# A new opening order, two more expert weight pieces ahead and other fillers in an attention and mixture-of-experts kernel

## The chip, the cores and the metric

The kernel runs on one core of one Trainium2 chip. The metric is the device time of one execution in microseconds. TensorE is PE in the profile, VectorE is DVE, ScalarE is ACT, GpSimd is POOL; SP issues the DMAs.

## The reference, cut to what matters

```python
# 1. chunked attention, 4 x 8 heads of 768 x 64: chunks of 32 queries, 16 keys of
#    left and 8 of right context and 8 memory keys
scores = scale * q_c @ k_full.T            # k_full = mem_k and the window
a = exp(scores - scores.max(-1)); a /= a.sum(-1) + 1e-9
out[chunk] = a @ v_full
# 2. heads side by side: x is 3072 tokens x 512
h = x @ w_in                               # 512 -> 2048
x = (h * sigmoid(h)) @ w_out               # 2048 -> 512
# 3. soft mixture of 8 experts with 4 slots each
logits = x @ phi                           # 512 -> 32 slots
d = exp(logits - logits.max(0)); d /= d.sum(0) + 1e-9      # over all tokens
slot_in = d.T @ x                          # 32 x 512
slot_out[e] = relu(slot_in[e] @ w1[e]) @ w2[e]             # 512 -> 1024 -> 512
c = exp(logits - logits.max(1)); c /= c.sum(1) + 1e-9      # over the slots
return c @ slot_out
```

## The kernel before, in words

The 3072 tokens are 24 groups of 128, and these are seven blocks of 256, 384, 384 and four times 512 tokens. Part 2 runs over steps (block j, slice f): `emit_h` makes 128 of the 2048 hidden values of a block (12 matmuls, in which weight and input are split into a high and a low part, L328), `g_tanh`, `g_mult`, `g_hi` and `g_lo` make the activation and its two parts on ACT and DVE, and `emit_y` adds the slice's share to the block's y (three matmuls for every 128 tokens, L357). Blocks 0 and 1 take turns in the first 32 steps, so step 2f is block 0 and 2f + 1 is block 1 with slice f; after that one block follows another. The two weights arrive in 16 slices with 512 KB each; `conv`, `conv_hi` and `conv_lo` (L189 to L222) bring them from a 64-bit layout into a high and a low fp32 part on ACT and DVE, in four operations and two.

The first 32 steps and the attention of the first groups are ordered by hand, word by word, in `OPENING` (L26). A word is a call with its arguments. `q.g`, `v.g`, `w.f.part`, `i` and `p` issue loads on SP's queue (608 KB for q, 512 KB for v and w, the constants, phi; part 0 is w_in and part 1 w_out). `c.f.s.parts` is one of the four conversion operations, `C` and `D` make the high and the low part. For group g, `S` are the scores (64 small matmuls), `M` the maxima and `U` their subtraction (DVE), `E` the exponential (ACT), `O` the sums and `N` the reciprocals (DVE), `Q` the product (POOL for p, DVE for v), `T` the four transposes, `A` their copy (ACT), `V` the values (64 small matmuls), `X` and `Y` the high and the low part (ACT, DVE). `h.i.bank`, `s.i`, `t.i`, `u.i`, `l.i`, `y.i` are the six parts of step i. `z.n.bank` are n filler matmuls. Every engine runs its own instructions in the order of the words, and so does SP with the loads: a load that waits for its buffer holds up the loads behind it. Groups 0 and 1 are block 0, groups 2 to 4 block 1, so step 1 needs V, X and Y of groups 2, 3 and 4 only.

The loads of groups 1 to 4 lie in the places that later take the weight slices: q.1 and v.1 in those of slices 14 and 13, q.2 and v.2 in 12 and 11, q.3 and v.3 in 10 and 9, q.4 and v.4 in 8 and 7 (`EARLY`, L137). The raw slice f is loaded to its own place (slice 0 to that of 15).

`keep_warm` (L172) issues filler matmuls into a bank that nothing reads; 21 of them stand ahead of the opening (L582), others around the last block's routing (L674 to L692).

`route` (L382) does the slot logits of a block, the running maximum and sum over the tokens, and adds d.T @ y to `acc`. For the last block it is spread over L626 to L702. There `c_turn` (L498) transposes four tiles of the combine weights into a bank and copies them back on ACT ("a") or DVE ("v"). `siz` is the slots' input, spread out for the experts. After it come the experts: `expert1` and `relu`, `to_hT`, `expert2`, `slot_out`, `combine` and the stores of the output.

The expert weights are 64 pieces with 512 KB, pieces 0 to 31 of w1 and 32 to 63 of w2. `load_ew` (L518) puts the next n of `ew_order` into a freed place, and `reload_ew` (L535) does that again as soon as the experts have read all of a place; when no piece is left the place goes to `ew_free`. During the last block the places are those of x0 (4 pieces, at its first step) and of the weight slices (2 each, one step after another); after its last step x1 (4), the last slices, two halved pieces in the activation buffers (`load_ew_halves`, L530) and st1 (2). That makes 44 pieces ahead of the experts.

Of the kernel before, what the change touches and what calls it, by code (L numbers as in the profile page):

```python
# [7 lines left out]
F32 = mybir.dt.float32  # L8
# [18 lines left out]
w.0.0 c.0.1.0 c.0.2.0 q.2 S.2.7.6 M.2 c.0.0.0 q.0 q.3 U.2 c.0.3.0 E.2 O.2 v.3 N.2 S.3.5.2 q.4 M.3 C.0.a.0 q.1 w.0.1  # L27
U.3 S.0.0.1 i S.4.7.6 v.2 E.3 M.0 S.1.5.2 O.3 w.1.0 N.3 U.0 c.0.1.1 M.4 Q.2.p U.4 w.1.1 E.0 T.2.0 A.2.a Q.3.p T.3.1
O.0 A.3.a M.1 N.0 c.0.0.1 E.4 V.3.0.7 U.1 O.4 V.2.6.1 E.1 N.4 c.1.1.0.1 w.3.1 v.4 v.1 X.3 Q.0.p Q.4.p T.4.5 c.1.0.0.1
T.0.2 O.1 v.0 N.1 A.4.a c.0.2.1 V.4.3.4 w.2.1 A.0.a Q.1.p w.2.0 c.0.3.1 T.1.5 Y.3 c.1.2.0.1 D.0.v.0 X.2 V.0.7.0 A.1.a  # L30
c.1.3.0.1 X.4 w.6.1 C.0.a.1 w.4.0 c.2.1.0.1 Y.2 C.1.a.0.1 V.1.2.5 Y.4 X.0 D.0.v.1 X.1 w.7.1 h.1.3 D.1.v.0.1 w.4.1
w.3.0 c.2.0.0.1 w.8.0 Y.1 h.3.4 w.13.0 s.1 Y.0 c.4.1.0.1 w.5.1 t.1 h.0.3 u.1 c.4.0.0.1 c.2.2.0.1 l.1.v w.8.1 s.3 s.0
w.5.0 c.2.3.0.1 t.0 y.1 w.6.0 h.2.3 C.2.a.0.1 t.3 u.3 D.2.v.0.1 u.0 c.3.1.0.1 l.0.v s.2 h.4.4 c.5.0.0.1 l.3.v t.2
c.3.2.0.1 c.4.2.0.1 h.5.3 u.2 c.3.0.0.1 w.7.0 l.2.v c.7.1.0.1 c.3.3.0.1 c.4.3.0.1 y.0 s.4 C.3.a.0.1 t.4 c.5.1.0.1 s.5
C.4.a.0.1 D.3.v.0.1 t.5 c.5.2.0.1 y.3 u.4 u.5 l.4.v l.5.v y.2 h.6.4 s.6 c.8.1.0.1 c.5.3.0.1 h.7.3 D.4.v.0.1 s.7
C.5.a.0.1 t.6 c.7.0.0.1 u.6 D.5.v.0.1 w.11.1 w.14.0 y.5 t.7 w.10.1 h.8.4 c.6.1.0.1 l.6.v s.8 y.4 w.15.1 w.9.0 h.10.3
w.11.0 c.7.2.0.1 u.7 t.8 v.5 u.8 l.7.v c.7.3.0.1 s.10 h.9.4 t.10 l.8.v c.6.0.0.1 c.8.0.0.1 s.9 w.10.0 y.6 u.10
C.7.a.0.1 c.6.2.0.1 h.11.3 c.6.3.0.1 q.5 c.10.1.0.1 t.9 y.8 C.6.a.0.1 D.7.v.0.1 l.10.v c.10.2.0.1 c.10.0.0.1 w.9.1
h.14.4 y.10 D.6.v.0.1 y.7 u.9 l.9.v c.8.2.0.1 s.11 t.11 w.14.1 w.12.0 h.12.3 c.10.3.0.1 u.11 c.11.1.0.1 s.12
c.8.3.0.1 l.11.v c.9.1.0.1 t.12 s.14 u.12 c.11.2.0.1 c.9.0.0.1 C.10.a.0.1 t.14 y.9 c.14.1.0.1 c.9.2.0.1 l.12.v h.13.3  # L40
c.9.3.0.1 s.13 w.12.1 D.10.v.0.1 h.15.4 C.8.a.0.1 u.14 y.11 t.13 u.13 h.21.3 l.13.v s.21 l.14.v C.9.a.0.1 D.8.v.0.1
t.21 y.12 u.21 c.14.2.0.1 h.16.3 s.15 c.11.0.0.1 t.15 y.13 c.11.3.0.1 h.17.4 w.13.1 l.21.v c.13.1.0.1 s.16 t.16 u.15
c.12.1.0.1 D.9.v.0.1 p C.11.a.0.1 l.15.v w.15.0 S.5.7.3 y.14 M.5 s.17 U.5 u.16 c.12.0.0.1 t.17 y.15 E.5 D.11.v.0.1
O.5 l.16.v h.18.3 u.17 h.20.4 l.17.v N.5 s.18 c.13.2.0.1 t.18 s.20 y.17 c.12.2.0.1 t.20 c.12.3.0.1 c.13.0.0.1 u.18
C.12.a.0.1 Q.5.p T.5.7 h.22.3 y.16 u.20 l.18.v h.19.4 s.22 A.5.v c.13.3.0.1 q.6 y.18 C.13.a.0.1 l.20.v s.19 t.22
V.5.7.3 t.19 c.15.1.0.1 h.23.4 D.12.v.0.1 c.14.0.0.1 u.19 y.20 c.15.2.0.1 X.5 l.19.v s.23 Y.5 c.14.3.0.1 t.23 u.22
y.19 D.13.v.0.1 u.23 C.14.a.0.1 S.6.7.3 c.15.0.0.1 l.23.v v.6 h.24.4 M.6 s.24 U.6 y.21 t.24 l.22.v E.6 h.26.3
D.14.v.0.1 O.6 u.24 c.15.3.0.1 s.26 h.25.4 l.24.v s.25 t.26 N.6 y.22 Q.6.v h.28.3 T.6.7 A.6.a u.26 C.15.a.0.1 t.25
q.7 h.27.4 l.26.v s.28 y.23 t.28 u.25 l.25.v s.27 t.27 V.6.7.3 y.24 u.28 X.6 D.15.v.0.1 Y.6 y.25 u.27 h.30.4 l.27.v
S.7.7.3 M.7 s.30 U.7 v.7 y.27 h.29.3 y.26 E.7 t.30 u.30 l.28.v O.7 h.31.4 s.29 N.7 Q.7.p t.29 T.7.7 u.29 A.7.a y.28  # L50
l.29.v s.31 t.31 u.31 l.31.v V.7.3.7 X.7 l.30.v Y.7 y.29
# [4 lines left out]
def attn_moe_softmoe_kernel(  # L56
# [12 lines left out]
    nc = tc.nc  # L69
# [38 lines left out]
    ident = cst[:, 0:128]  # L108
# [6 lines left out]
    warm = [call[:, 0:4].rearrange("p t s -> p (t s)").bitcast(mybir.dt.bfloat16)]  # L115
# [3 lines left out]
    def bank(b, shape, name):  # L119
        if b is None:  # L120
            return mbank(shape, name)
        return psum.tile(shape, F32, tag=f"b{b}", name=name)
# [49 lines left out]
    def keep_warm(n, b=0):  # L172
        pw = bank(b, [128, 256], "ps_warm")
        for _ in range(n):
            nc.tensor.matmul(pw, warm[0][:, 0:128], warm[0], start=True, stop=True)
# [331 lines left out]
    ew_order = [*range(28, 32), *range(28), *range(32, 64)]  # L507
# [70 lines left out]
    with tc.manual_schedule():  # L578
        nc.vector.memset(call[:, 0:4], 0.0)
        nc.vector.memset(s_run, 0.0)  # L580
        nc.scalar.activation(out=s_run, in_=s_run, func=ACTF.Exp)
        keep_warm(21)  # L582
# [14 lines left out]
        warm[0] = ident.bitcast(mybir.dt.bfloat16)  # L597
# [5 lines left out]
        for i in range(step_of[2, 0], len(steps)):  # L603
            j, f = steps[i]
            if f == 2 and j < 4:
                misc[0] = [5, 6, 7] if j == 2 else [6, 7]
            if j == NB - 1 and f == 0:
                lctx.close()
                c4_p = ctx.enter_context(tc.tile_pool(name="c4", bufs=1, side="right", reuse_waits="tile"))
                c4.append(c4_p.tile([128, NT, 128], F32R, name="c4"))  # L610
                load_ew((x_p, "x0", 4))
            emit_h(i, 3 + i % 2)
            run(2 * i)
            g_tanh(i)
            g_mult(i)
            g_hi(i)
            g_lo(i, "v")
            emit_y(i - LAG, (0, 1, 2) if i == len(steps) - 1 else None)
            if j == NB - 1 and LAG <= f < NF - 1:
                load_ew((wring, f"w{f - LAG}", 2))  # L620
            run(2 * i + 1)
        assert not slots
        L = NB - 1
# [20 lines left out]
        load_ew((wring, f"w{NF - 1}", 2))  # L644
        load_ew_halves(("gl", {}), ("gl", {}))
        load_ew_halves(("gl", {}), ("g", {"bufs": 2}))
        nc.scalar.activation(out=y[:, 3, 0:256], in_=y_t[L][3][:, 0:256], func=ACTF.Copy, scale=0.5)
# [23 lines left out]
        siz = [g_p.tile([128, 2, 8, 32], F32, tag="gh", name="siz") for _ in range(2)]  # L671
        for t in siz:
            nc.gpsimd.memset(t, 0.0)
        route(L, 4, lambda: (c_turn(8, 1, "a"), c_turn(12, 2, "a"), keep_warm(5, 1)))  # L674
        route(L, 5)
        c_turn(16, 4, "v")
        keep_warm(2, 1)
# [10 lines left out]
        keep_warm(5, 4)  # L688
        psi = mbank([128, 4, 32], "ps_si")
        for c in range(4):  # L690
            nc.tensor.matmul(psi[:, c], acc[:, 128 * c:128 * c + 128], seln, start=True, stop=True)
        keep_warm(4, 4)  # L692
        for c in range(4):
            nc.vector.tensor_copy(
                out=bass.AP(
                    tensor=siz[c // 2].tensor, offset=siz[c // 2][:, c % 2].offset, ap=[siz[c // 2].ap[0], [36, 8], [1, 4]]
                ),
                in_=psi[:, c].rearrange("p (e s) -> p e s", e=8),
            )
# [85 lines left out]
        to_hT(0, hs0, st_tile(2, [128, 8, 128], F32, "hT"))  # L785
# [5 lines left out]
        pool, tag, _ = ew_free.pop(0)  # L791
        to_hT(1, hs1, pool.tile([128, 8, 128], F32, tag=tag, name="hT"))
# [87 lines left out]
```

## Time and profile before

| | us |
|---|---|
| median of 3 runs | 711.75 (710.59 to 714.34) |
| profiled execution, its own time | 713.54 |
| span in its trace | 711.7 |
| PE busy | 686.2 (96%), 6445 matmuls |
| DVE, ACT, POOL busy | 335.3, 251.9, 32.2 |
| mean granted clock of TensorE | 0.972 |
| moved by DMA | 85.29 MB, mean 120 GB/s |

The page cuts the span into forty equal slices and gives each engine's busy share in tenths: TensorE is at 9 from the third slice to the last but one. Matmuls are pipelined and their ends modelled, so a busy TensorE is not one at its peak. The granted clock stands beside, 1.00 for 2.4 GHz and 0.50 for 1.2 GHz. The chain of waits is followed back from the last instruction: each piece is what the next one had to wait for, and "issue" is time in which an engine waited for nothing that the profile shows. In the timeline the brackets give the idle time before an instruction and what ended it.

### The profile page before, as it was taken

What the parts mean: (1) busy time and instruction counts of PE and PEld (TensorE: products, weight loads), DVE (VectorE), ACT (ScalarE), POOL (GpSimd) and SP (SyncE); (2) the same over time, 40 slices, a digit from 0 to 9 for tenths busy, and PEclk for the clock granted to TensorE, in tenths of its full rate; (3) what the DMA queues carried; (4) which work ended last, traced back from release to release, by engine and by line L of the source; (5) the groups of instructions that cost most, each with busy time, mean ns of one, the idle gap of its engine ahead of it and who ended that gap; (6) DMA issues with size and microseconds to landing.
All of it is one profiled execution on the core that took longest, in us unless ns stands there. A gap on an engine that the chain in (4) does not pass through costs nothing.

```text
span 711.7 us, 14737 instructions
## 1 busy us (share of the span) xinstructions
PE 686.2 (96%) x6445; PEld 551.7 (78%) x6445; DVE 335.3 (47%) x667; ACT 251.9 (35%) x475; POOL 32.2 (5%) x41
## 2 busy tenths in 40 slices
PE   6799999999999999999999999999999999999993
PEld 4699988888888877788887788887788878786452
DVE  5679888444545344433434533434443333324222
ACT  3588666333333232222332222333222323223113
POOL 1100010000000000000000000000000001000000
PEclk7589999999999999999999999999999999999997
DMA  9797012021222211201201201111112245569998
GB/s 355 294 383 316 1 36 67 30 66 37 65 67 66 66 30 36 67 30 36 66 30 36 66 30 52 50 46 50 38 31 88 73 152 181 181 211 330 369 397 269
DMA packets 27760, 85.29 MB, mean 120 GB/s; under 512 B 2608, under 2 KB 9008, under 8 KB 27696
## 3 DMA queue, kind: packets, MB, share of 16 engines
q1 hardware_dynamic: 27696, 84.36, 33.8%
q8 instruction: 50, 0.82, 0.5%
q14 instruction: 14, 0.11, 0.0%
HBM read 78.05 MB, written 6.29 MB: 119 GB/s over the span
## 4 chain that ended last, share of the span: by engine, by line
PE 95%; DVE 1%; issue 1%; DMA 1%; ACT 0%; POOL 0%; DVEq 0%; SPq 0%; ACTq 0%; POOLq 0%
PE ps_h L336 38%; PE ps_y L366 13%; PE ps_y L367 12%; PE ps_y L370 12%; PE ps_x L305 4%; PE ps_s L239 3%; PE ps_o L742 2%; PE ps_e L710 2%; PE ps_t L287 2%; PE ps_yt L402 1%; PE ps_a L469 1%; PE ps_f L772 1%; PE ps_l L411 1%; DMA early<-in_qk_dram 1%; PE ps_r L423 0%
## 5 line engine op out<-in xcount | busy, mean ns | idle before, releaser
L336 PE MATMUL ps_h<-xbuf,w 128*128 128x512 f32 (+2 forms) x1344 | 287.0, 364 | 0.0
L336 PEld LDWEIGHTS ps_h<-xbuf,w 128*128 128x128 f32 x1344 | 235.4, 190 | 35.1 <-issue 2.7
L366 PE MATMUL ps_y<-w,gh 128*128 128x512 f32 x384 | 155.5, 405 | 0.0
L367 PE MATMUL ps_y<-w,gh 128*128 128x512 f32 x384 | 150.4, 392 | 0.0
L347 DVE SCALAR_TENSOR_TENSOR g<-g,ps_h 128x512 f32<-128x512 f32 (+2 forms) x112 | 68.0, 608 | 130.2 <-ACT g L343 129.8
L370 PE MATMUL ps_y<-w,gl 128*128 128x512 f32 x384 | 106.2, 390 | 0.0
L343 ACT ACTIVATE g<-ps_h 128x512 f32<-128x512 f32 (+2 forms) x112 | 60.0, 536 | 110.3 <-PE ps_h L336 106.8
L184 DVE TENSOR_TENSOR gl<-g,gh 128x512 fp32r<-128x512 f32 (+2 forms) x112 | 68.3, 614 | 63.6 <-ACT gh L179 61.9
L179 ACT ACTIVATE gh<-g 128x512 fp32r<-128x512 f32 (+2 forms) x112 | 63.7, 570 | 81.0 <-DVE g L347 73.9
L366 PEld LDWEIGHTS ps_y<-w,gh 128*128 128x128 f32 x384 | 72.1, 188 | 20.8 <-issue 6.5
L370 PEld LDWEIGHTS ps_y<-w,gl 128*128 128x128 f32 x384 | 72.1, 188 | 15.5
L367 PEld LDWEIGHTS ps_y<-w,gh 128*128 128x128 f32 x384 | 72.3, 188 | 12.9
L184 POOL TENSOR_TENSOR a<-a,smm 128x512 f32<-128x512 f32 x19 | 20.6, 1086 | 496.0 <-DVE smm L277 369.0
L321 DVE TENSOR_TENSOR xbuf<-ps_x,xbuf 128x256 fp32r<-128x256 f32 x48 | 18.1, 418 | 45.2 <-ACT xbuf L179 45.1
L179 ACT ACTIVATE xbuf<-ps_x 128x256 fp32r<-128x256 f32 x48 | 15.7, 384 | 48.2 <-PE ps_x L305 48.2
L179 ACT ACTIVATE at<-ps_t 128x512 f32<-128x512 f32 x19 | 11.3, 596 | 50.6 <-PE ps_t L287 50.6
L269 ACT ACTIVATE a<-a 128x512 f32<-128x512 f32 x20 | 12.6, 629 | 43.6 <-DVE a L263 28.4
L247 DVE TENSOR_REDUCE mx<-ps_s 128x4 f32<-128x256 f32 x48 | 18.1, 418 | 20.6 <-PE ps_s L239 20.5
L305 PEld LDWEIGHTS ps_x<-at,v 64*64 64x64 f32 x1280 | 21.3, 139 | 7.0 <-issue 4.8
L305 PE MATMUL ps_x<-at,v 64*64 64x32 f32 x1280 | 23.5, 224 | 0.0
L205 DVE SCALAR_TENSOR_TENSOR raw<-raw 128x1024 uint32<-128x1024 uint32 (+1 forms) x17 | 20.0, 1181 | 3.8 <-ACT raw L201 3.8
L184 DVE TENSOR_TENSOR w<-wx,w 128x1024 fp32r<-128x1024 f32 (+1 forms) x17 | 19.7, 1156 | 2.8 <-ACT w L179 2.7
(131 smaller groups left out, 475.4 us busy)
## 6 DMA issues: line engine op xcount, KB each, us to landing
ew<-in_w_dram SPq DMA_DIRECT2D x62, 512.0 KB, 6.1
qk<-in_qk_dram SPq DMA_DIRECT2D x20, 608.0 KB, 3.9
v<-in_v_dram SPq DMA_DIRECT2D x20, 512.0 KB, 3.4
raw<-in_win_dram SPq DMA_DIRECT2D x16, 512.0 KB, 9.9
raw<-in_wout_dram SPq DMA_DIRECT2D x16, 512.0 KB, 10.4
out_dram<-ob SPq DMA_DIRECT2D x9, 512.0 KB, 5.5
early<-in_qk_dram SPq DMA_DIRECT2D x4, 608.0 KB, 7.8
early<-in_v_dram SPq DMA_DIRECT2D x4, 512.0 KB, 10.1
```

Of the source, the lines that this page charges most:

```text
L179: nc.scalar.activation(out=out, in_=in_, func=ACTF.Copy)
L184: (nc.gpsimd if eng == "p" else nc.vector).tensor_tensor(**kw)
L205: nc.vector.scalar_tensor_tensor(out=lo_w, in0=hi_w, scalar=0x80000000, in1=lo_w, op0=ALU.bitwise_and, op1=ALU.bitwise_or)
L239: nc.tensor.matmul(ps[r][q, p], t[h, p, q], t[h, p, w:w + 64], start=True, stop=True)
L247: nc.vector.tensor_reduce(out=mx[:, 4 * r:4 * r + 4], in_=ps_t[g][r], axis=AX.X, op=ALU.max)
L305: nc.tensor.matmul(px[s][h, u, q], vt[k, n, c], AT[k, n, q], start=True, stop=True)
L336: nc.tensor.matmul(ph, w[:, wi, 128 * c:128 * c + 128], x[:, c, :], start=(c == 0 and m == 0), stop=(c == 3 and m == 2),)
L343: nc.scalar.activation(out=g_t[i], in_=h_t[i], func=ACTF.Tanh, scale=0.5)
L347: nc.vector.scalar_tensor_tensor(out=g, in0=g, scalar=1.0, in1=h_t.pop(i), op0=ALU.add, op1=ALU.mult)
L366: nc.tensor.matmul(y_t[j][t], gh[:, r], w[:, 0], start=(f == 0), stop=False)
L367: nc.tensor.matmul(y_t[j][t], gh[:, r], w[:, 1], start=False, stop=False)
L370: nc.tensor.matmul(y_t[j][t], gl[:, r], w[:, 0], start=False, stop=(f == NF - 1))
```

## The change

1. `OPENING` is another order of the same words (some with another bank or engine), with two fillers added (`z.12.3` and `z.4.4`). The scores now run 3, 2, 4, 0, 1 and the transposes 2, 3, 4, 1, 0; V.0 and V.1 stand behind `h.1.3`, where all five values stood ahead of it. The loads begin q.3, q.2, w.0.1, q.4, q.0, w.0.0. `p` stands near the end.
2. A filler has 512 columns, where it had 256; 10 stand ahead of the opening, where 21 stood. The zeroed strip that feeds them is twice as wide.
3. Piece 27 is loaded at the last block's first step, into the place st2, and one more piece goes in halves into a g and a gh buffer, so 46 pieces are ahead of the experts. `siz` is allocated and zeroed earlier. The transposed hidden values of both expert halves share one freed place (the first half's had st2).
4. Around the last routing the copies of c_turn 8 and 12 go to DVE, the fillers are 2, 2 and 1 (they were 5, 2, 5 and 4) and lie in other banks, and the slots' input comes out in two banks, where it had one.

The opening is cut to its first lines; behind them the same words follow in another order.

```diff
@@ -24,31 +24,31 @@
 NEG = -3.0e38
 OPENING = """
-w.0.0 c.0.1.0 c.0.2.0 q.2 S.2.7.6 M.2 c.0.0.0 q.0 q.3 U.2 c.0.3.0 E.2 O.2 v.3 N.2 S.3.5.2 q.4 M.3 C.0.a.0 q.1 w.0.1
-U.3 S.0.0.1 i S.4.7.6 v.2 E.3 M.0 S.1.5.2 O.3 w.1.0 N.3 U.0 c.0.1.1 M.4 Q.2.p U.4 w.1.1 E.0 T.2.0 A.2.a Q.3.p T.3.1
-O.0 A.3.a M.1 N.0 c.0.0.1 E.4 V.3.0.7 U.1 O.4 V.2.6.1 E.1 N.4 c.1.1.0.1 w.3.1 v.4 v.1 X.3 Q.0.p Q.4.p T.4.5 c.1.0.0.1
-T.0.2 O.1 v.0 N.1 A.4.a c.0.2.1 V.4.3.4 w.2.1 A.0.a Q.1.p w.2.0 c.0.3.1 T.1.5 Y.3 c.1.2.0.1 D.0.v.0 X.2 V.0.7.0 A.1.a
-c.1.3.0.1 X.4 w.6.1 C.0.a.1 w.4.0 c.2.1.0.1 Y.2 C.1.a.0.1 V.1.2.5 Y.4 X.0 D.0.v.1 X.1 w.7.1 h.1.3 D.1.v.0.1 w.4.1
-w.3.0 c.2.0.0.1 w.8.0 Y.1 h.3.4 w.13.0 s.1 Y.0 c.4.1.0.1 w.5.1 t.1 h.0.3 u.1 c.4.0.0.1 c.2.2.0.1 l.1.v w.8.1 s.3 s.0
-w.5.0 c.2.3.0.1 t.0 y.1 w.6.0 h.2.3 C.2.a.0.1 t.3 u.3 D.2.v.0.1 u.0 c.3.1.0.1 l.0.v s.2 h.4.4 c.5.0.0.1 l.3.v t.2
-c.3.2.0.1 c.4.2.0.1 h.5.3 u.2 c.3.0.0.1 w.7.0 l.2.v c.7.1.0.1 c.3.3.0.1 c.4.3.0.1 y.0 s.4 C.3.a.0.1 t.4 c.5.1.0.1 s.5
-C.4.a.0.1 D.3.v.0.1 t.5 c.5.2.0.1 y.3 u.4 u.5 l.4.v l.5.v y.2 h.6.4 s.6 c.8.1.0.1 c.5.3.0.1 h.7.3 D.4.v.0.1 s.7
...
+q.3 S.3.7.6 q.2 w.0.1 q.4 q.0 S.2.5.2 c.0.1.1 w.0.0 M.3 S.4.0.1 U.3 E.3 M.2 S.0.7.6 i q.1 c.0.2.1 U.2 M.4 O.3 E.2
+c.0.0.1 O.2 U.4 c.0.0.0 w.1.1 N.3 c.0.1.0 E.4 M.0 N.2 Q.2.p U.0 Q.3.p v.2 O.4 T.2.5 E.0 w.1.0 A.2.a c.0.2.0 S.1.2.0
+N.4 c.0.3.0 M.1 O.0 v.3 U.1 Q.4.p c.1.0.0.1 c.1.1.0.1 c.1.2.0.1 T.3.1 N.0 A.3.a V.2.7.6 w.2.1 T.4.5 E.1 A.4.a w.2.0
+v.4 z.12.3 V.4.2.0 O.1 X.2 Y.2 w.4.1 C.0.a.0 v.1 N.1 Q.0.p V.3.1.5 v.0 Q.1.p c.2.1.0.1 D.0.v.0 w.3.1 c.1.3.0.1 X.4
+Y.4 T.1.7 T.0.6 X.3 Y.3 A.0.a C.1.a.0.1 c.0.3.1 c.2.0.0.1 C.0.a.1 z.4.4 h.1.3 A.1.a s.1 c.2.2.0.1 V.0.2.0 V.1.6.5 X.0
+w.3.0 D.1.v.0.1 c.2.3.0.1 t.1 h.3.4 w.5.1 X.1 w.10.1 u.1 Y.0 Y.1 w.6.0 w.5.0 c.3.1.0.1 l.1.v s.3 w.4.0 D.0.v.1
+c.3.2.0.1 C.2.a.0.1 t.3 h.0.3 D.2.v.0.1 s.0 c.4.1.0.1 t.0 u.3 c.3.0.0.1 l.3.v y.1 c.4.2.0.1 u.0 h.2.4 s.2 t.2 l.0.v
+h.5.3 c.5.1.0.1 w.13.1 c.4.0.0.1 c.3.3.0.1 w.6.1 h.4.4 u.2 c.5.2.0.1 s.4 y.0 l.2.v c.5.0.0.1 s.5 t.4 w.7.0 c.4.3.0.1
+y.3 C.3.a.0.1 D.3.v.0.1 u.4 t.5 w.7.1 y.2 C.4.a.0.1 w.8.1 u.5 h.7.4 D.4.v.0.1 c.6.1.0.1 c.7.1.0.1 l.4.v l.5.v
+c.5.3.0.1 q.5 h.6.3 s.7 s.6 t.7 u.7 t.6 C.5.a.0.1 c.7.2.0.1 y.4 w.12.1 w.8.0 l.7.v h.8.4 u.6 s.8 w.14.1 h.9.3
...
 """
@@ -112,7 +112,7 @@
     call = const.tile([128, NT, 32], F32, name="call")
     acc = const.tile([128, 512], F32, name="acc")
     s_run = const.tile([128, 1], F32, name="s_run")
-    warm = [call[:, 0:4].rearrange("p t s -> p (t s)").bitcast(mybir.dt.bfloat16)]
+    warm = [call[:, 0:8].rearrange("p t s -> p (t s)").bitcast(mybir.dt.bfloat16)]
 
     misc = [[6, 7], 0]
 
@@ -170,7 +170,7 @@
         nc.sync.dma_start(out=phi_sb, in_=phi)
 
     def keep_warm(n, b=0):
-        pw = bank(b, [128, 256], "ps_warm")
+        pw = bank(b, [128, 512], "ps_warm")
         for _ in range(n):
             nc.tensor.matmul(pw, warm[0][:, 0:128], warm[0], start=True, stop=True)
 
@@ -504,7 +504,7 @@
 
 
     c4, ew_t, ew_free, ew_used = [], {}, [], {}
-    ew_order = [*range(28, 32), *range(28), *range(32, 64)]
+    ew_order = [*range(28, 32), 27, *range(27), *range(32, 64)]
 
     def ew_dma(m, halves):
         src = (w1 if m < 32 else w2)[m // 2 % 16, :, 2 * (m % 2):2 * (m % 2) + 2]
@@ -576,10 +576,10 @@
     at(2 * step_of[NB - 1, NF - 1], c_parts, 16)
 
     with tc.manual_schedule():
-        nc.vector.memset(call[:, 0:4], 0.0)
+        nc.vector.memset(call[:, 0:8], 0.0)
         nc.vector.memset(s_run, 0.0)
         nc.scalar.activation(out=s_run, in_=s_run, func=ACTF.Exp)
-        keep_warm(21)
+        keep_warm(10)
         ops = {
             "q": load_qk, "v": load_v, "w": load_w, "i": load_cst, "p": load_phi,
             "c": conv, "C": conv_hi, "D": conv_lo,
@@ -594,7 +594,7 @@
         load_v(8)
 
         nc.vector.tensor_copy(out=selr, in_=sel)
-        warm[0] = ident.bitcast(mybir.dt.bfloat16)
+        warm[0] = cst.bitcast(mybir.dt.bfloat16)
 
         def run(i):
             for fn, args in slots.pop(i, []):
@@ -609,6 +609,7 @@
                 c4_p = ctx.enter_context(tc.tile_pool(name="c4", bufs=1, side="right", reuse_waits="tile"))
                 c4.append(c4_p.tile([128, NT, 128], F32R, name="c4"))
                 load_ew((x_p, "x0", 4))
+                load_ew((st_p, "st2", 1))
             emit_h(i, 3 + i % 2)
             run(2 * i)
             g_tanh(i)
@@ -642,8 +643,12 @@
             copy("av"[c % 2], yT[:, c, 0:384], pt)
         emit_y(last[2], (3,))
         load_ew((wring, f"w{NF - 1}", 2))
+        siz = [g_p.tile([128, 2, 8, 32], F32, tag="gh", name="siz") for _ in range(2)]
+        for t in siz:
+            nc.gpsimd.memset(t, 0.0)
         load_ew_halves(("gl", {}), ("gl", {}))
         load_ew_halves(("gl", {}), ("g", {"bufs": 2}))
+        load_ew_halves(("g", {"bufs": 2}), ("gh", {}))
         nc.scalar.activation(out=y[:, 3, 0:256], in_=y_t[L][3][:, 0:256], func=ACTF.Copy, scale=0.5)
         nc.vector.tensor_scalar(out=y[:, 3, 256:512], in0=y_t[L][3][:, 256:512], scalar1=0.5, scalar2=None, op0=ALU.mult)
         c_turn(0, 0, "a")
@@ -668,13 +673,9 @@
             nc.tensor.matmul(pr[:, r], sel, lp[:, r], start=True, stop=True)
         rt[L, "pr"], rt[L, "y"] = pr, y
         misc[0] = [5, 6, 7, 0]
-        siz = [g_p.tile([128, 2, 8, 32], F32, tag="gh", name="siz") for _ in range(2)]
-        for t in siz:
-            nc.gpsimd.memset(t, 0.0)
-        route(L, 4, lambda: (c_turn(8, 1, "a"), c_turn(12, 2, "a"), keep_warm(5, 1)))
+        route(L, 4, lambda: (c_turn(8, 1, "v"), c_turn(12, 2, "v"), keep_warm(2, 4)))
         route(L, 5)
         c_turn(16, 4, "v")
-        keep_warm(2, 1)
         rs = sm_p.tile([128, 1], F32, tag="sb", name="rs")
         nc.vector.tensor_scalar(out=rs, in0=s_run, scalar1=1e-9, scalar2=None, op0=ALU.add)
         nc.vector.reciprocal(out=rs, in_=rs)
@@ -685,17 +686,17 @@
         dl = rt[L, "dl"]
         for t in range(BLOCKS[L] // 128):
             nc.tensor.transpose(pd[:, t], dl[32:64, 128 * t:128 * t + 128], ident[32:64, 32:64])
-        keep_warm(5, 4)
-        psi = mbank([128, 4, 32], "ps_si")
+        keep_warm(2, 2)
+        psi = [bank(b, [128, 2, 32], "ps_si") for b in (1, 3)]
         for c in range(4):
-            nc.tensor.matmul(psi[:, c], acc[:, 128 * c:128 * c + 128], seln, start=True, stop=True)
-        keep_warm(4, 4)
+            nc.tensor.matmul(psi[c // 2][:, c % 2], acc[:, 128 * c:128 * c + 128], seln, start=True, stop=True)
+        keep_warm(1, 2)
         for c in range(4):
             nc.vector.tensor_copy(
                 out=bass.AP(
                     tensor=siz[c // 2].tensor, offset=siz[c // 2][:, c % 2].offset, ap=[siz[c // 2].ap[0], [36, 8], [1, 4]]
                 ),
-                in_=psi[:, c].rearrange("p (e s) -> p e s", e=8),
+                in_=psi[c // 2][:, c % 2].rearrange("p (e s) -> p e s", e=8),
             )
         slot_scores(L, pd)
         route(L, 7)
@@ -782,14 +783,15 @@
         hs0 = relu(0, ph0)
         ph1 = [bank(2 + hf, [128, 512], "ps_e") for hf in range(2)]
         expert1(1, range(2), ph1)
-        to_hT(0, hs0, st_tile(2, [128, 8, 128], F32, "hT"))
+        pool, tag, _ = ew_free.pop(0)
+        hT = pool.tile([128, 2, 8, 128], F32, tag=tag, name="hT")
+        to_hT(0, hs0, hT[:, 0])
         c_turn(NT - 4, 6, "v")
         expert1(1, range(2, 4), ph1)
         hs1 = relu(1, ph1)
         po = bank(0, [128, 256], "ps_o")
         expert2(po, 0, 0, range(4))
-        pool, tag, _ = ew_free.pop(0)
-        to_hT(1, hs1, pool.tile([128, 8, 128], F32, tag=tag, name="hT"))
+        to_hT(1, hs1, hT[:, 1])
         sp = g_p.tile([128, 256], F32, tag="g", name="sp", bufs=2)
         so_t = g_p.tile([128, 2, 256], F32R, tag="gl", name="so")
         expert2(po, 0, 0, range(4, 8))
```

## Rows read from the trace of the kernel before

**Rows 1.** Chain of waits, whole span: start us, us, what.

```profile
12.53 2.60 issue
...
17.23 1.47 PE ps_t L287 x6
18.70 2.69 issue
...
26.29 1.38 issue
...
36.46 7.88 PE ps_h L336 x36
```

**Rows 2.** Timeline of PE, 0 to 45 us: start us, us, instructions [idle before].

```profile
1.05 4.66 PE L175 MATMUL ps_warm<-call 128*128 128x256 bf16 x21 [1.05 <-DVE s_run L580]
5.94 1.09 PE L239 MATMUL ps_s<-early 64*32 64x64 f32 x64 [0.22 <-DMA early<-in_qk_dram]
9.10 0.86 PE L239 MATMUL ps_s<-early 64*32 64x64 f32 x64 [2.07 <-DMA early<-in_qk_dram]
...
11.97 0.55 PE L239 MATMUL ps_s<-early 64*32 64x64 f32 x9 [1.16 <-DVE mx L247]
15.13 2.10 PE L239 MATMUL ps_s<-early 64*32 64x64 f32 x119 [2.60 <-issue]
...
22.66 3.62 PE L305 MATMUL ps_x<-early 64*64 64x32 f32 x125 [0.69 <-ACT early L179]
...
44.18 0.40 PE L366 MATMUL ps_y<-w,gh 128*128 128x512 f32 x1
```

**Rows 3.** The page, part 3: DMA queues.

```profile
q8 instruction: 50, 0.82, 0.5%
```

**Rows 4.** DMA queues from 12 to 13 us.

```profile
q8 instruction: 1, 0.02, 6.7%
```

**Rows 5.** Windows of the opening, as their head line names them, clock after POOL.

```profile
10.00:12.00 2.00, 0.84 (x64) 0.63 (x46) 1.97 (x8) 0.35 (x1) 1.04 (x1) 0.55 1.02 423
...
30.00:32.00 2.00, 2.00 (x65) 1.94 (x66) 2.00 (x4) 1.15 (x3) 0.00 (x0) 0.50 0.00 0
```

**Rows 6.** Windows of line 336: PE, PEld, clock, DMA share, GB/s.

```profile
40.40:42.40 2.00, 2.00 (x11) 2.00 (x11) 0.87 0.91 305
```

**Rows 7.** Timeline of DVE, opening.

```profile
10.26 0.70 DVE L247 TENSOR_REDUCE mx<-ps_s 128x4 f32<-128x256 f32 x2
...
12.20 0.60 DVE L251 TENSOR_REDUCE mx<-ps_s 32x4 f32<-32x192 f32 x2
```

**Rows 8.** Timeline of POOL, opening.

```profile
10.49 1.04 POOL L184 TENSOR_TENSOR early<-early,smm 128x512 f32<-128x512 f32 x1 [10.05 <-DVE smm L277]
```

**Rows 9.** Chain of waits, later places at full clock.

```profile
94.63 2.11 PE ps_h L336 x12
...
112.86 1.06 PE ps_x L305 x64
```

**Rows 10.** Window of 50 to 60 us: PE, PEld, DVE, ACT, POOL, clock, DMA.

```profile
50.00:60.00 10.00, 10.00 (x56) 9.05 (x56) 10.00 (x13) 7.82 (x12) 0.00 (x0) 1.00 1.03 410
```

**Rows 11.** Timeline of PE, last routing.

```profile
655.16 0.71 PE L175 MATMUL ps_warm<-cst 128*128 128x256 bf16 x5 [1.57 <-ACT c L179]
...
660.23 10.51 PE L710 MATMUL ps_e<-ew,siz 128*32 128x512 f32 x96
```

**Rows 12.** Timeline of DVE, last routing.

```profile
656.92 0.69 DVE L181 CAST c<-ps_c 128x512 fp32r<-128x512 f32 x1 [1.42 <-PE ps_c L501]
657.53 0.14 DVE L679 TENSOR_SCALAR rs<-s_run 128x1 f32<-128x1 f32 x1
...
658.06 0.86 DVE L476 SCALAR_TENSOR_TENSOR acc<-acc,al,ps_a 128x256 f32<-128x256 f32 x2
```

**Rows 13.** Waits of PE's weight loads, 640 to 712 us: total, times, longest.

```profile
PEld ps_e L710 <- DMA ew<-in_w_dram: 0.3, 1, 0.3
```

**Rows 14.** Waits of PE, 28 to 640 us (the only one).

```profile
PE ps_t L287 <- POOL a L184: 0.3, 1, 0.3
```

## What the change should do: the prediction

> **What bounds the kernel now.** I read the page's slices first (TensorE is full in all but the first two of the forty and the last), then the chain of waits over the whole span, then TensorE's timeline in the first 45 us and in the last 60. The chain is TensorE almost everywhere; only the opening and the last routing have holes in it. In the opening the chain has three pieces called "issue", 2.60, 2.69 and 1.38 us, in which TensorE waits for nothing that is shown [rows 1]. Their places are the clue. Counted in matmuls by the timeline, the first falls after 21 fillers, three score groups of 64 and 9 of the fourth, that is 222; the second after 119 + 6 more, at 347; the third after 2 + 125 more, at 474 [rows 1, 2]. So one comes every 125 to 127 matmuls. The page has an instruction queue with 50 packets and 0.82 MB [rows 3]: 16 KB each, and TensorE's 12,890 instructions (a weight load and a matmul each) divided by 50 are 258, or 129 matmuls. One such packet stands in each of the stretches 12 to 13, 18 to 19, 25 to 26 and 28 to 29 us and in no other before 36; one row is shown [rows 4]. I read the holes as TensorE at the end of a block of instructions while the next one is under way. If a block is asked for when the block before it is entered, the first hole's was asked for at matmul 96 (222 less 126), the 11th of the second score group, at about 9.2. Then the three latencies are 15.13 - 9.2 = 5.9, 21.39 - 15.13 = 6.3 and 27.66 - 21.39 = 6.3 us, nearly one constant, while the data transfers fill the DMA engines (share 1.02 [rows 5]). In that stretch TensorE can't run faster than 126 matmuls in 6.2 us, and the attention of the five early groups is 5 x (64 + 4 + 64) matmuls.
>
> The second loss is the clock: a mean of 0.55 from 10 to 12 us puts its fall from 1.00 to 0.50 (2.4 to 1.2 GHz) at about 10.2 [rows 5], and one of 0.87 from 40.4 to 42.4 puts its return at 40.9, 4.5 us after dense h matmuls began at 36.4 [rows 6]. The transposes and values from 28 to 36 keep TensorE busy with small tiles and did not raise it [rows 5].
>
> **The change part by part. The opening's order.** The number to compare is the start of y.1, the first y matmul: 44.18 us before [rows 2]. In both orders the same matmuls precede it (the five groups' scores, transposes and values, h.1, h.3, h.0), but the new one adds 16 fillers. I walk TensorE's new queue (all times are estimates). Ten fillers of 512 columns: 21 of 256 took 4.66, so 0.44 each, 1.1 to 5.5. q.3 is now the first load: 1.24 MB took until 9.10 - 5.94 = 3.16 [rows 2], so 0.39 MB/us, and 0.62 MB are there before 5.5. S.3 and S.2 to 7.5. Matmul 96 is now 10 + 64 + 22, in S.2 at 6.8; the block at 222, the 20th of S.0, is ready at 13.0. S.0's operand is the fifth transfer, 10.7, so a hole of some 2 us stays there; S.0 ends at 13.7. DVE's M.0 follows with 0.70 + 0.60, N.2 with two small ones of about 0.2 [rows 7], POOL's product takes 1.04 [rows 8]: T.2 at 16.6. T.2 0.5, S.1 1.1, T.3 0.5: 18.7. V.2 crosses 347 in its ninth matmul; that block is ready at 13.0 + 6.2 = 19.2. V.2 at half clock costs 64 x 3.62/125 = 1.85: 20.8. T.4: 21.3.
>
> Now z.12, twelve fillers: at half clock 5.3 us, but if the clock comes back 4.5 us after they began, ten go at 0.44 and two at 0.22: 4.9 and the end at 26.2. V.4 crosses 474 there, ready at 19.2 + 6.2 = 25.4: no hole. At full clock V.4 and V.3 cost 1.06 each, not 1.85 [rows 9]; T.1 and T.0 0.8; z.4 0.9: h.1.3 starts at 30.0, takes 2.11 [rows 9], 32.1. Only now come V.0 and V.1; the block at 600, V.0's 30th matmul, is ready at 27.1 + 6.2 = 33.3, a hole of 0.7; they end at 34.9. h.3.4 2.11 and h.0.3 1.4 (two thirds of it): y.1 at 38.4, with a few hops 38.6. That is 5.6 us earlier. Where it comes from: the holes shrink from 6.7 us to about 3, and h.1, h.3 and h.0 at full clock save 7.88 - 5.6 = 2.3, four of the five V's another 3.2; the fillers take 5.8 of it back, and the rest is waiting for loads and softmaxes that the order now fills.
>
> What could be late next: DVE. After M.0 its queue to Y.3 holds about 13 us in my count (U.0, O.4, M.1, O.0, U.1, O.1 at 0.7 to 0.9, two half conversions and D.0 at 0.7, two whole ones at 1.2, three Y at 0.74, the small ones): 15.0 to 29.4, against 30.0 on TensorE; 0.6 of slack, so the term is good to about 1 us. The moved loads: v.4 is the 15th transfer, at about 22.5 for a use at 26; SP passes its first blocked issue (w.13.1, behind V.1 in v.1's place) only at some 27, where w.7.1 blocked it before; p (phi) goes to the queue's end behind v.7, and its first use is in the routing after the opening: nothing. The wider memset adds 0.1.
>
> **After y.1** the work is the same and TensorE is the limit; a lead of 5.6 us is kept if the weight conversions keep up. DVE is full in one stretch, 10.00 of 10 us in 50 to 60 [rows 10], but waits elsewhere, and the new order has it busy in the first 30 us. I take nothing off; the other end is the whole 5.6.
>
> **Two more weight pieces.** 1.05 MB leave the stretch in which the DMA engines are full, 2.6 us of their time at 0.39 MB/us. TensorE's waits for weights there are 0.3 us, twice; one row is shown [rows 13]. So the gain is 0 to 0.6 and I take 0: the pieces only keep this so when the experts start earlier. The first runs at the last block's start, where nothing waits for it; the second waits for the last gh tile and SP's queue with it, until the last y is through with that tile. hT goes into a freed place; 24 pieces have been read by then.
>
> **Fillers around the last routing.** Now five fillers stand behind c_turn in its own bank and wait 1.57 us for ACT's copy, with the d transposes queued behind them [rows 11]. After: two wide ones in a bank already copied, and the copies on DVE. So d can be transposed 1.3 us earlier. But DVE then has two copies of 0.69 in front of dl's, as wide, then s_run, the third copy of 0.69, the three small ones that were between 657.5 and 658.1, and acc's 0.86 [rows 12]: from 653.8 that ends at 658.1, not 658.9. Then the slot inputs 0.8 and one filler 0.2 in place of four at 0.11: experts at 659.2, not 660.23 [rows 11]. Gain 1.0 (0.5 if DVE's copies cost more there, 1.4 if the two banks let the copies begin after half of the products). Behind it everything waits on the experts, so the end moves with it.
>
> The sum: 713.54 of the profiled execution (711.7 of span and 1.8 around it) less 5.6 less 1.0 is 706.9. The median of the runs, 711.75, is 1.8 below that execution; from it the same 6.6 give 705.2, which I forecast.
>
> **A rule of the Trainium skill against this.** In this trace TensorE stops three times with a fetch packet in the data's way [rows 1, 4]. The Trainium skill, "Runtime: NRT & Kernel Launch", section "Instruction fetch mechanics", says that instructions stream in 16 KiB blocks of 256, which agrees with 0.82 MB in 50 packets, but also that crossing a block is mostly hidden, because dispatch is slower than the fill. By that the holes would have another cause; the trace speaks against it where the DMA engines are full. It makes the third rival below.
>
> **The rivals.** *The fetch is slower than 6.2 us*, since the new order leaves the DMA engines no pause in the first 35 us: at 7.5 us a block S.0, V.2 and V.0 each wait longer, y.1 comes at 42.3, gain 1.9 + 1.0: 708.8. For it: a queue never empty; against: three latencies within 0.4 us at full DMA. *DVE starves TensorE later*: PE waits in 45 to 80 us and half to all of the 5.6 goes: 708 to 711. For it the full stretch [rows 10]; against: TensorE's longest wait for another engine from 28 to 640 us was 0.3 [rows 14]. *The holes are no fetch* and stay, 6.7 in place of 3: 3.7 more, 708.9. Against: the packets and the count. *The clock, on the other side:* z.12 does not raise it, or the V's behind lose it again. Then z.12 costs 5.3, V.4 and V.3 3.7, the transposes 1.0, z.4 1.8, h.1.3 at 33.1 takes 3.8, V.0 and V.1 3.7, and h.3 and h.0 at half clock 6.4: y.1 at 47.0, 2.8 late, less 1.0 of the tail: 713.5, slower than 711.75. It decides where V.4 runs at 1.85. For it: TensorE's clock did not rise in 8 us of small tiles; against: it did in 4.5 us of dense ones, and z.12 is dense for longer.
>
> **How the numbers follow.** Forecast 0.62 (own range 702.5 to 708), slow fetch 0.10, DVE 0.12, no fetch 0.06, clock 0.10. The range 702.5 to 711.5 leaves out the clock's case and a few hundredths below. What a measurement of this kernel can tell is about 0.5%, 3.6 us: below 708.2 lie the forecast and half of the middle cases, 0.72; above 715.3 only the worst of the clock's case with another, 0.07; 0.21 between.
>
> **What would show it.** Right: y.1 near 38.6, the clock at 1.00 before V.4, holes only in S.0 and V.0 and under 3 us together, and the experts' first matmul 1 us earlier against the last yt transposes. Wrong: V.4 at 1.85 us; a hole over 3 us in S.0; h or y waiting for DVE between 45 and 80 us, so that the lead at block 2's first h is under 5 us; TensorE waiting for dl or acc behind DVE's copies longer than before; an expert matmul that waits for its weights.

## The result, and the profile after

| | before | after |
|---|---|---|
| median of the runs, us | 712.38 (710.59 to 714.34, 4 runs) | 705.06 (704.83 to 705.58, 4 runs) |
| ratio after to before | | 0.9898, 95% interval 0.987 to 0.9926 |
| profiled execution, its own time, us | 713.54 | 704.83 |
| span in its trace, us | 711.7 | 702.4 |
| mean granted clock | 0.972 | 0.989 |

7.3 us less by the medians, against the 6.6 forecast; 9.3 less between the two traced spans. The forecast of 705.2 holds, but by the traces the opening gave more and the tail a little more than its terms. The pair of traces shows more than the medians, in part because the traced execution of the kernel before was 1.2 us above its median.

TensorE's timeline of the changed kernel, opening (start us, us, instructions, and in brackets the idle time before them; `...` marks rows left out):

```profile
1.19 3.68 PE L175 MATMUL ps_warm<-call 128*128 128x512 bf16 x10 [1.19 <-DVE s_run L580]
...
6.40 0.86 PE L239 MATMUL ps_s<-early 64*32 64x64 f32 x64 [0.75 <-DMA early<-in_qk_dram]
9.53 0.85 PE L239 MATMUL ps_s<-early 64*32 64x64 f32 x64 [2.27 <-DMA early<-in_qk_dram]
12.33 1.28 PE L239 MATMUL ps_s<-qk 64*32 64x64 f32 x64 [1.95 <-DMA qk<-in_qk_dram]
16.46 1.11 PE L287 MATMUL ps_t<-cst,early 128*128 128x128 f32 x4 [2.86 <-POOL early L184]
...
22.03 2.54 PE L175 MATMUL ps_warm<-call 128*128 128x512 bf16 x11
24.50 2.09 PE L305 MATMUL ps_x<-early 64*64 64x32 f32 x128
...
28.12 2.44 PE L336 MATMUL ps_h<-xbuf,w 128*128 128x384 f32 x12
...
36.16 0.40 PE L366 MATMUL ps_y<-w,gh 128*128 128x512 f32 x1
```

The last row answers to the end of [rows 2]: the first y matmul, y.1, starts at 36.16, not 44.18, so 8.02 us are gained by then. No bracket in this stretch says "issue", where [rows 1, 2] had three such holes. What TensorE waits for now has names: loads (0.75, 2.27, 1.95) and POOL's product, 2.86 before the transposes of group 2.

Between the two ends the same work takes the same time. Windows from y.1 to the first transposes of the last block's y (us, then busy time and matmuls of PE, PEld, DVE, ACT, POOL, clock, DMA share, GB/s), before and after:

```profile
44.20:646.40 602.20, 601.83 (x5168) 493.85 (x5167) 286.85 (x557) 213.79 (x404) 25.16 (x30) 1.00 0.24 80
```

```profile
36.20:638.40 602.20, 601.82 (x5168) 493.93 (x5167) 285.71 (x556) 214.56 (x406) 24.10 (x29) 1.00 0.24 83
```

Both are 602.20 us with 5168 matmuls, TensorE busy and at full clock all through. So the lead of the opening is neither lost nor added to, and the rest is the tail. TensorE there, after:

```profile
638.39 1.47 PE L642 MATMUL ps_yt<-cst,y 128*128 128x128 f32 x12
...
645.45 0.38 PE L175 MATMUL ps_warm<-cst 128*128 128x512 bf16 x1
646.61 0.43 PE L442 MATMUL ps_d<-cst,dl 32*128 32x32 f32 x4 [0.78 <-ACT dl L431]
...
650.95 10.51 PE L711 MATMUL ps_e<-ew,siz 128*32 128x512 f32 x96
...
688.31 3.56 PE L773 MATMUL ps_f<-so,c 128*128 128x256 f32 x24 [0.60 <-DVE so L757]
```

From the first yt transpose to the first expert matmul it is 650.95 - 638.39 = 12.56 us; before, it was 660.23 [rows 11] less the 646.37 of this row, 13.86:

```profile
646.37 1.47 PE L641 MATMUL ps_yt<-cst,y 128*128 128x128 f32 x12
```

That is 1.30 less. From the experts to the last output matmuls both have 37.3 to 37.4 us (to 688.31 here), and 14.1 from there to the end of the span. 8.02 + 1.30 is the whole 9.3. DVE's queue in the last routing ended as worked out, with two copies ahead and acc 0.87 wide as in [rows 12]:

```profile
645.78 1.29 DVE L181 CAST c<-ps_c 128x512 fp32r<-128x512 f32 x2
...
649.20 0.87 DVE L476 SCALAR_TENSOR_TENSOR acc<-acc,al,ps_a 128x256 f32<-128x256 f32 x2
```

### The profile page after: what moved, and what is told of

Same layout as the page of the kernel before. It is cut to its first block, busy times and chain, and to the rows that moved or that the text cites. A ratio compares the mean times of both kernels' runs of the same rounds, so it can differ in the third digit from the quotient of the medians.

```text
span 702.4 us, 14734 instructions
## 1 busy us (share of the span) xinstructions
PE 680.2 (97%) x6436; PEld 543.5 (77%) x6439; DVE 336.5 (48%) x669; ACT 251.6 (36%) x474; POOL 31.4 (4%) x40
## 4 chain that ended last, share of the span: by engine, by line
PE 95%; DVE 1%; DMA 1%; issue 0%; POOL 0%; SPq 0%; ACT 0%; DVEq 0%; POOLq 0%; ACTq 0%
PE ps_h L336 38%; PE ps_y L366 13%; PE ps_y L367 12%; PE ps_y L370 12%; PE ps_x L305 4%; PE ps_s L239 2%; PE ps_o L743 2%; PE ps_e L711 2%; PE ps_t L287 2%; DMA qk<-in_qk_dram 1%; PE ps_yt L402 1%; PE ps_f L773 1%; PE ps_a L469 1%; PE ps_l L411 1%; PE ps_warm L175 1%
## 5 line engine op out<-in xcount | busy, mean ns | idle before, releaser
L179 ACT ACTIVATE at<-ps_t 128x512 f32<-128x512 f32 x20 | 11.9, 596 | 51.7 <-PE ps_t L287 51.7
L269 ACT ACTIVATE a<-a 128x512 f32<-128x512 f32 x20 | 12.6, 630 | 44.9 <-DVE a L263 28.6
L239 PEld LDWEIGHTS ps_s<-qk 64*32 64x32 f32 x1280 | 14.3, 107 | 8.4 <-issue 8.0
## 6 DMA issues: line engine op xcount, KB each, us to landing
raw<-in_wout_dram SPq DMA_DIRECT2D x16, 512.0 KB, 10.1
early<-in_v_dram SPq DMA_DIRECT2D x4, 512.0 KB, 10.7
```

What stands on the lines that cost most here:

```text
L179: nc.scalar.activation(out=out, in_=in_, func=ACTF.Copy)
L239: nc.tensor.matmul(ps[r][q, p], t[h, p, q], t[h, p, w:w + 64], start=True, stop=True)
```

## The experiments

All were compared with runs of the kernel before on the same chip. Labels stand in brackets.

**The order alone** (order_alone): the new `OPENING` in the kernel before, with the two new fillers taken out and 21 narrow ones kept. The cut shows what the order lacks against the changed kernel's.

```diff
-v.4 z.12.3 V.4.2.0 O.1 X.2 Y.2 w.4.1 ...
+v.4 V.4.2.0 O.1 X.2 Y.2 w.4.1 ...
-... C.0.a.1 z.4.4 h.1.3 A.1.a ...
+... C.0.a.1 h.1.3 A.1.a ...
```

> The kernel before with the new order of the opening alone: no z.12 and z.4, the 21 narrow fillers ahead, the old tail. Theory (the order does it, by meeting the ends of the instruction blocks where TensorE waits for something else anyway): y.1 starts at 35.5 to 37.5 us, not 44.2, there is no issue hole over 0.5 us before it, the tail is as before, and the time is 5.5 to 8 us less than before. Rival (the added fillers do it, by bringing the clock back): y.1 at 39 to 42, V.4 at half clock (1.85 us for its 64 matmuls), and no more than 4 us gained.

Measured: 707.79, ratio 0.9933 (0.9918 to 0.9947), by which it is 4.8 us less (3.8 to 5.8). Its opening:

```profile
10.59 0.50 PE L239 MATMUL ps_s<-qk 64*32 64x64 f32 x9 [0.66 <-DMA qk<-in_qk_dram]
12.93 1.10 PE L239 MATMUL ps_s<-qk 64*32 64x64 f32 x55 [1.83 <-issue]
...
24.09 3.64 PE L305 MATMUL ps_x<-early 64*64 64x32 f32 x128 [1.85 <-DVE smm L276]
...
38.10 0.40 PE L366 MATMUL ps_y<-w,gh 128*128 128x512 f32 x1
```

y.1 is at 38.10, 6.1 us earlier, between the theory's 35.5 to 37.5 and the rival's 39 to 42. One "issue" of 1.83 us stands in S.0 after 9 matmuls, which is the 222nd again (21 + 192 + 9), where the theory allowed none over 0.5. The time moved less than expected (5.5 to 8), though the interval reaches into that range, and V.4 and V.3 ran at half clock (3.64 for both), as the rival had it. So the order does most, and neither theory holds whole.

**The tail alone** (tail_alone): the changed kernel with the old `OPENING` and 21 fillers of 256 columns.

```diff
-    def keep_warm(n, b=0):
+    def keep_warm(n, b=0, cols=512):
...
-        keep_warm(10)
+        keep_warm(21, 0, 256)
```

> The changed kernel with the old opening and its 21 narrow fillers, so the edits of the tail alone (pieces, copies on DVE, wide fillers, two banks). Theory: y.1 at 44.2 as before, and from the first yt transpose to the first expert matmul 12.6 us in place of 13.9: 1.0 to 1.4 us gained. Rival (the tail's end is set by the stores and the weight transfers): the experts start earlier, but the end does not move by more than 0.5 us.

Measured: 711.66, ratio 0.9969 (0.9954 to 0.9983), by which it is 2.2 us less (1.2 to 3.3), and 12.56 us from the yt transposes to the experts. The end moved with them (51.45 us from the first expert matmul to the end of the span, 51.47 before); the rival falls. y.1 is at 43.64, 0.5 earlier than before. The two parts, 4.8 and 2.2, make up nearly all of the 7.3. In the opening the holes stand where they stood [rows 2], to the matmul:

```profile
11.94 0.56 PE L239 MATMUL ps_s<-early 64*32 64x64 f32 x9 [0.87 <-DVE mx L247]
15.04 2.12 PE L239 MATMUL ps_s<-early 64*32 64x64 f32 x119 [2.54 <-issue]
```

**Without the fillers of the opening** (no_z): the changed kernel without `z.12.3` and `z.4.4`.

> The changed kernel without z.12 and z.4. Theory (the next block of instructions, ready at about 25, holds V.4 anyway, and the clock is back before z.12 begins): V.4 ends within 0.5 us of where it ended, z.4's 0.8 us are saved, the time is from 1.2 us less to 0.3 more. Rival (the fillers keep the clock up over the wait for the block): the clock is at 0.50 in V.3 or in h.1.3, y.1 1.5 to 5 us later, the time 1.5 to 5 us more than with them.

Measured: 705.48 (705.01 to 706.19), ratio 0.9896 (0.9881 to 0.9911): the time of the changed kernel. Timeline of TensorE, and windows with the clock:

```profile
10.71 0.61 PE L239 MATMUL ps_s<-qk 64*32 64x64 f32 x20 [0.66 <-DMA qk<-in_qk_dram]
13.25 0.94 PE L239 MATMUL ps_s<-qk 64*32 64x64 f32 x44 [1.93 <-issue]
...
24.03 3.56 PE L305 MATMUL ps_x<-early 64*64 64x32 f32 x128 [1.64 <-DMA early<-in_v_dram]
...
29.15 3.39 PE L336 MATMUL ps_h<-xbuf,w 128*128 128x384 f32 x12
```

```profile
21.00:22.00 1.00, 1.00 (x47) 0.96 (x43) 1.00 (x3) 1.00 (x3) 0.00 (x0) 0.89 1.02 406
22.00:24.00 2.00, 0.39 (x4) 0.15 (x2) 1.97 (x6) 1.62 (x6) 1.04 (x1) 1.00 1.04 412
24.00:25.00 1.00, 0.97 (x48) 1.00 (x51) 0.96 (x5) 1.00 (x2) 0.45 (x1) 0.82 0.99 385
...
26.00:28.00 2.00, 2.00 (x59) 1.94 (x56) 1.61 (x3) 0.79 (x4) 0.00 (x0) 0.50 1.01 403
```

The clock was back at about 21.2 (a mean of 0.89 from 21 to 22) without either new filler and fell again at about 24.6 (0.82 from 24 to 25), after TensorE had stood for 1.64 us ahead of V.4. V.4, V.3 and h.1.3 paid for it (3.56 for the two, 3.39 for h.1.3, 2.4 in the changed kernel): the rival's picture. But z.12 and z.4 are not paid either: y.1 is at 38.09, and the time is the same. The fillers buy the clock for about what they cost; that they gain anything is not shown.

**Without the two pieces** (no_pieces): `ew_order`, the places of hT and the two loads as before.

```diff
-    ew_order = [*range(28, 32), 27, *range(27), *range(32, 64)]
+    ew_order = [*range(28, 32), *range(28), *range(32, 64)]
...
-                load_ew((st_p, "st2", 1))
...
-        load_ew_halves(("g", {"bufs": 2}), ("gh", {}))
...
```

> The changed kernel with the old order of the expert pieces, 44 of them ahead of the experts and the old places for hT. Theory (TensorE didn't wait for weights before, and the experts start only 1.3 us earlier): the time is within 0.6 us. Rival (the pieces are what lets the earlier experts run): expert matmuls wait for their weights, and 1.0 to 2.6 us are lost.

Measured: 706.29 (704.88 to 707.26), ratio 0.9906 (0.9891 to 0.9921). This is not apart from the changed kernel's 0.9898, and the trace shows nothing that the pieces did: 12.56 us from the yt transposes to the experts and 37.4 from there to the last output matmuls, as with them, and one wait of 0.3 us for a weight. Its opening has the changed kernel's code, and yet y.1 is at 39.20:

```profile
23.17 4.23 PE L175 MATMUL ps_warm<-call 128*128 128x512 bf16 x12
27.33 2.07 PE L305 MATMUL ps_x<-early 64*64 64x32 f32 x128
```

z.12 took 4.2 us here against 2.5 above, because the clock came back at 26.2, not at 21.0. This is the size of what one profiled execution can mislead by.

**The fetch by itself** (tiny_both): 512 small matmul calls in the form of the scores, into two free banks, behind h.0.3 and again in block 3, slice 4. TensorE runs each call as two matmuls, as it does with the scores, so each place has 1024.

```diff
+    def tiny(n, *bs):
+        pw = [bank(b, [128, 64], "ps_k") for b in bs]
...
+                    nc.tensor.matmul(pw[r][32 * c:32 * c + 32], src[h, 0:32], src[h, 64:128], start=True, stop=True)
```

> The changed kernel with 512 extra small matmuls (form of the scores, 64 x 32 weights, 64 columns, some 11 ns each at full clock) in two places: behind h.0.3, where the DMA engines are full of weight slices until about 52 us, and in the step of block 3 with slice 4, where they are nearly idle. Theory (a block of 256 instructions is fetched by DMA when the one before it is entered, behind the data): in the first place TensorE stops every 126 to 128 matmuls, and the blocks are entered 5.9 to 6.7 us apart as long as the transfers fill the engines; in the second it stops just as often, but the blocks are 2.5 to 4 us apart. Rival (the holes belong to the attention's own dependences): no hole in either place, 512 in 5 to 9 us.

Measured: 773.43 us in a single execution, which is not compared in time. The first place, where the DMA engines' share is 1.01 to 1.03 from 40 to 60 us, 0.66 from 60 to 65 and 0.02 after that:

```profile
43.51 2.04 PE L184 MATMUL ps_k<-call 64*32 64x64 f32 x128 [3.12 <-issue]
49.70 2.04 PE L184 MATMUL ps_k<-call 64*32 64x64 f32 x128 [4.16 <-issue]
55.90 2.04 PE L184 MATMUL ps_k<-call 64*32 64x64 f32 x128 [4.15 <-issue]
62.09 2.04 PE L184 MATMUL ps_k<-call 64*32 64x64 f32 x128 [4.16 <-issue]
65.82 2.04 PE L184 MATMUL ps_k<-call 64*32 64x64 f32 x128 [1.69 <-issue]
69.55 2.04 PE L184 MATMUL ps_k<-call 64*32 64x64 f32 x128 [1.69 <-issue]
```

The blocks begin 6.19, 6.20 and 6.19 us apart while the data run, then 3.73. The second place, with idle DMA engines:

```profile
307.52 2.04 PE L184 MATMUL ps_k<-cst 64*32 64x64 f32 x128 [2.53 <-issue]
311.53 2.04 PE L184 MATMUL ps_k<-cst 64*32 64x64 f32 x128 [1.96 <-issue]
314.98 2.04 PE L184 MATMUL ps_k<-cst 64*32 64x64 f32 x128 [1.41 <-issue]
```

Every 128 matmuls again, 3.45 to 4.01 us apart over its seven blocks. The rival (no hole) falls: these matmuls depend on nothing, and they stop all the same. The trace's records of the instruction packets show the cause. With the DMA engines full a packet starts 3.6 to 3.7 us after TensorE has entered the block before it, with idle engines 1.0 to 1.7 us after; the packet itself takes 0.9 to 1.5 us in both places, and TensorE goes on 1.2 to 1.6 us after it has landed. So the holes are the fetch of TensorE's instructions, one block ahead, and the data in front of it cost 2.2 to 2.7 us a block.

**Group 2 ahead of group 0** (swap), to see whether POOL's 2.86 us were the limit.

```diff
-... E.4 M.0 N.2 Q.2.p U.0 ...
+... E.4 N.2 Q.2.p M.0 U.0 ...
-... O.0 v.3 U.1 ...
+... O.0 v.3 v.4 U.1 ...
```

> The changed kernel with N.2 and Q.2 ahead of M.0, so that T.2 doesn't stand behind the maxima of group 0, and v.4 loaded two transfers earlier. Theory (in the opening TensorE then goes from block end to block end): T.2 starts 1.3 us earlier, but V.4's 56th matmul waits for its block, ready 12.3 to 12.9 us after the block with S.0's 20th was entered, so y.1 comes only 0 to 1 us earlier and the time is 0 to 1 us less. Rival (the wait for POOL's product was what set the opening): y.1 1.3 to 2.8 us earlier, the time 1.3 us or more less.

Measured: 705.63 (705.07 to 706.89), ratio 0.9894 (0.9873 to 0.9915): no change from the changed kernel's 0.9898. The timeline says why:

```profile
14.35 1.11 PE L287 MATMUL ps_t<-cst,early 128*128 128x128 f32 x4 [1.11 <-POOL early L184]
...
18.98 1.01 PE L305 MATMUL ps_x<-early 64*64 64x32 f32 x55 [0.77 <-issue]
...
25.18 1.29 PE L305 MATMUL ps_x<-early 64*64 64x32 f32 x73 [1.07 <-issue]
...
28.01 2.44 PE L336 MATMUL ps_h<-xbuf,w 128*128 128x384 f32 x12
...
31.82 0.71 PE L305 MATMUL ps_x<-at,v 64*64 64x32 f32 x34 [0.78 <-issue]
```

T.2 starts 2.1 us earlier, and TensorE then stops in V.2 after 9, in V.4 at the 56th and in V.0 after 30 matmuls: the 347th, 474th and 600th, where the prediction had put the ends of the blocks. They begin at 18.98, 25.18 and 31.82. y.1 is at 37.01, not earlier but 0.85 later than in the changed kernel's first profile; the theory's 0 to 1 us earlier is not met.

**Copies on ACT again** (copies_act): c_turn 8 and 12 of the changed kernel with "a" for "v".

> The changed kernel with c_turn 8 and 12 copied by ACT as before; the wide fillers in their other bank stay. Theory (what cost time was the fillers' wait for their own bank's copy): from the first yt transpose to the first expert matmul 12.3 to 12.8 us, as with DVE's copies (12.56), since DVE's queue and ACT's then end nearly alike. Rival (the copies on ACT held d and so the slots' sums): 13.3 us or more.

Measured: 705.96, ratio 0.9889 (0.9866 to 0.9912), and 651.19 - 638.82 = 12.37 us to the experts: the copies on DVE cost 0.2 rather than gain. The two traces of combined, below, have 12.38 with the copies on ACT; the six traces with them on DVE and two banks (after, after_again, tail_alone, no_z, no_pieces, swap) have 12.56.

**One argument of the kernel before** (bank_only).

```diff
-        route(L, 4, lambda: (c_turn(8, 1, "a"), c_turn(12, 2, "a"), keep_warm(5, 1)))
+        route(L, 4, lambda: (c_turn(8, 1, "a"), c_turn(12, 2, "a"), keep_warm(5, 4)))
```

> The kernel before with one argument changed: the five narrow fillers behind c_turn 8 and 12 go to bank 4, not to bank 1, whose copy they waited for. Theory (that wait is what the tail lost): from the first yt transpose to the first expert matmul 12.6 to 13.2 us, not 13.86. Rival (the narrower gain is in the other fillers and the two banks): 13.6 us or more.

Measured: 712.56, ratio 0.9984 (0.9969 to 0.9999).

```profile
646.95 1.47 PE L641 MATMUL ps_yt<-cst,y 128*128 128x128 f32 x12
...
654.01 0.71 PE L175 MATMUL ps_warm<-cst 128*128 128x256 bf16 x5
655.17 0.43 PE L442 MATMUL ps_d<-cst,dl 32*128 32x32 f32 x4 [0.45 <-ACT dl L431]
...
659.66 5.79 PE L710 MATMUL ps_e<-ew,siz 128*32 128x512 f32 x52
```

659.66 - 646.95 = 12.71 us to the experts: 1.15 of the tail's 1.30 is this one wait. By the time of the whole kernel the gain is barely clear of noise. The five fillers run at 654.01 without a pause, where [rows 11] had 1.57 us in front of them.

**The slots' input in one bank** (one_bank), the changed kernel otherwise.

```diff
-        psi = [bank(b, [128, 2, 32], "ps_si") for b in (1, 3)]
+        psi = bank(1, [128, 4, 32], "ps_si")
...
```

> The changed kernel with the slots' input in one bank, as before. Theory (the first two copies then wait for all four products): the experts start 0.2 to 0.4 us later than the 12.56 after the first yt transpose. Rival (the last copy and the filler set it anyway): 12.5 to 12.7.

Measured: 706.60 (705.28 to 707.77), ratio 0.9903 (0.9887 to 0.9918); 653.56 - 640.79 = 12.77 us to the experts, 0.2 more.

**What the runs point to** (combined): the order of swap, without `z.4.4`, with the copies on ACT.

> The order with N.2 and Q.2 ahead of M.0 and v.4 earlier, without z.4, and with c_turn 8 and 12 copied by ACT. Theory (the opening goes from block end to block end, so only z.4's 0.5 us and the copies' 0.2 are to be had): 0 to 1 us below the changed kernel, which this measurement can't tell from nothing. Rival (z.4 holds the clock into h.1.3): h.1.3 in part at half clock and 1 us or more lost.

Measured: 704.59 (704.11 to 706.33), ratio 0.9881 (0.9863 to 0.9899). In its opening V.0 stops later by the four fillers of z.4 that are gone, after 34 matmuls in place of swap's 30, which is the 600th again:

```profile
30.17 0.77 PE L305 MATMUL ps_x<-at,v 64*64 64x32 f32 x34
31.50 0.60 PE L305 MATMUL ps_x<-at,v 64*64 64x32 f32 x28 [0.57 <-issue]
```

Since the time is not apart from the changed kernel's, both were run once more on one chip.

> The changed kernel once more, to stand on the same chip beside the next one. Theory (TensorE's clock comes back at one of two moments, before or in z.12, 4 to 6 us apart): its executions spread over 704.5 to 707.5 us, and y.1 of the profiled one is at 36.0 to 36.6 or at 38.3 to 39.3. Rival (the first profile's 36.2 is the rule): all within 0.6 us of 705.

> The combined version beside the changed kernel on one chip. Theory (both go from block end to block end): 0 to 1.2 us less than the changed kernel, intervals overlapping. Rival (the earlier T.2 and the dropped z.4 count in full): 1.5 us or more less.

Measured: the changed kernel 706.00 (704.55 to 707.35), ratio 0.9898 (0.9883 to 0.9914), y.1 at 36.50; combined 704.73 (704.47 to 704.86), ratio 0.9876 (0.9862 to 0.9889), y.1 at 36.78. It beats the kernel before; against the changed one its median is 1.3 us lower in this comparison and the intervals overlap, so that it is faster is likely, not shown.

## Why the prediction held, step by step

**The holes are fetches: right.** Three kernels with the old opening stop at the matmuls 222, 347 and 474; the new order stops at 222 after 9 of S.0 with 21 fillers and after 20 of S.0 with 10 (no_z, no_pieces); with swap it stops at 347, 474 and 600. The count fits and no group does. The packets' own times settle it: in the kernel before three instruction packets start at 12.6, 18.9 and 25.1 us and take 1.07 us each (the 6.7% of [rows 4]), and TensorE goes on 1.4 to 1.5 us after each has landed, at 15.13, 21.39 and 27.66. In twelve traces, with tiny_both, all 37 "issue" holes at the end of a block, of 0.19 us and more, end 1.25 to 1.63 us after such a packet. In the changed kernel the packets still start 6.0 to 6.3 us apart (10.1, 16.3, 22.3, 28.4, 34.7), so the fetch is no faster; the order lets other waits cover it. The latency of 6.2 us is met at 6.19 in tiny_both. The Trainium skill ("Runtime: NRT & Kernel Launch", section "Instruction fetch mechanics") calls a crossing mostly hidden; here it cost up to 4.2 us where matmuls are small and the DMA engines full, and the measurement decides.

**TensorE's walk to h.1.3: right in place, wrong in one size.** T.2 was put at 16.6 and came at 16.46, V.2 at 19.2 and came at 19.67, z.12 at 21.3 and came at 22.03. The hole put into S.0, some 2 us, is there in no_pieces (1.98); in the profiled execution q.0 landed later (S.0 at 12.33, not 10.7) and took its place. The step that was mis-sized is "4.9 and the end at 26.2": z.12 took 2.5 and ended at 24.5, because the clock was at 1.00 from 21.0 on:

```profile
20.00:21.00 1.00, 1.00 (x49) 1.00 (x44) 0.75 (x3) 1.00 (x2) 0.00 (x0) 0.50 1.02 406
21.00:22.00 1.00, 0.98 (x28) 0.86 (x26) 0.52 (x1) 1.00 (x3) 0.00 (x0) 0.99 1.04 414
...
24.00:26.00 2.00, 2.00 (x105) 1.58 (x105) 1.97 (x5) 1.37 (x3) 1.50 (x2) 1.00 1.04 416
```

So z.12 took 2.4 us less than its term. Since it began 0.7 later it ended 1.7 earlier than walked, and the rest of the 2.4 between 8.0 and 5.6 is smaller: the hole of 0.7 put into V.0 is not there (0.3 in after_again), against 0.3 more for h.1.3. In the execution of no_pieces the clock came back in z.12 as forecast, though 3.0 us after its start and not 4.5, z.12 took 4.2, and y.1 came at 39.2, 5.0 us earlier, near the forecast 38.6. Six traces of this opening have the return at 19.7, 20.1 and 21.0 (after_again, copies_act, after) or at 25.5 to 26.2 (one_bank, tiny_both, no_pieces); swap has it at 18.2, and combined, in its two traces, at 23.3 and 23.8. So the forecast walked a late return and the profile showed an early one; the changed kernel's runs in after_again spread over 2.8 us. What sets the moment is open.

**The number: closer than its terms.** The forecast subtracted its 6.6 from a median of three runs, 711.75. With the fourth run the median before is 712.38, 0.6 higher, and the gain by the medians is 0.7 more than forecast. The two cancel, so that 705.2 stands beside 705.06 is in part luck.

**Where the gain lies.** I gave the holes some 3.7 us and the clock 5.5, less 5.8 for fillers. In the profiled executions TensorE's idle time up to y.1 fell from 11.9 to 9.0 us only (the brackets of the two timelines), for named waits took the holes' place. From start to start, the values of five groups fell from 9.4 to 5.7, the three h from 7.8 to 6.0, scores and transposes by some 1.5; fillers rose by 1.9. So the larger part is work at 2.4 GHz that was done at 1.2, and it came by the order too, since h.1 stands 8 us earlier and the late values stand behind it. How much of the 8.0 the fetch alone gives isn't shown: no run changes the fetch without the order, and each hole less also moves the clock.

**DVE does not starve TensorE: right**, by the two windows of 602.20 us. **The clock's case** did not come in any of six traces; no_z and order_alone show a part of it, V.4 and V.3 at half clock (3.56 and 3.64), but the clock is back before h.3 there and y.1 comes at 38.1, far from the rival's 47.0. **The pieces: right**, nothing (their 1.05 MB are 2.7 us at 0.39 MB/us, not the 2.6 of the prediction, which changes nothing). **The tail: right in sum (1.0, measured 1.30)**, but part of its account was empty: the bank gave 1.15 and the two banks 0.2, and the copies on DVE, which I took for part of the gain, cost 0.2.

## What to carry to other kernels

A hole called "issue" that returns after the same number of instructions, whatever they are, was an instruction fetch here: count instructions between holes and look for the instruction packets in the DMA queues before looking for a dependence, and lay the waits that can't be avoided over the ends of the blocks. Whether fewer, wider matmuls there would help by themselves was not tested. A filler should go to a bank that nobody is copying; here it waited 1.57 us for one. And where the clock's return moves from one execution to the next, one profile of each kernel can be 3 us off in a stretch (y.1 at 36.16 and at 39.20 with one opening): look at several before crediting an edit.

## What the runs showed that was not expected

The clock can come back while only small tiles run. The prediction took from [rows 5] that transposes and values did not in 8 us; with the new order scores, transposes and values from 16.5 to 21 us did, in order_alone and no_z too (about 21.1 and 21.2, without z.12 in either). They did not always: in one_bank, tiny_both and no_pieces the same work ended with the clock still at 0.50, and it came back only in z.12. What tells the two apart is open. After a return without z.12 it fell again, at 24.5 in order_alone and at 24.6 in no_z, where TensorE had stood for 1.85 and 1.64 us ahead of V.4.
